# Another set of assumed latencies for the list scheduler of a two-layer attention and MLP kernel, and a condition and a priority in its tail

One Trainium2 chip, one core. The metric is the device time of the whole program in microseconds (us), the median of several executions; lower is better. The profile is of one execution and gives a span some 1.8 us shorter than that execution's device time.

## The reference

Two layers, each attention and then an MLP, on one sequence of 2048 tokens of width 512; 32 heads of 16; hidden width 1792; all tensors bf16.

```python
def _A_ref(x, wqkv, wo):                       # H = 32, Dh = 16
    qkv = (x @ wqkv).reshape(B, S, 3, H, Dh)...
    p = softmax(einsum("bhqd,bhkd->bhqk", q, k) * Dh ** -0.5)
    return einsum("bhqk,bhkd->bhqd", p, v)... @ wo
def _B_ref(x, w1, b1, w2, b2):
    return gelu(x @ w1 + b1) @ w2 + b2          # tanh approximation

x = x + _A_ref(_layernorm(x), A_wqkv, A_wo)     # and _B_ref, both twice
```

Scores are 2 layers x 32 heads x 2048 x 2048, that is 4096 blocks of 128 keys x 512 queries, and each element needs an exponential. That is what the kernel is built around.

## The kernel before

The kernel is a program that writes a program. Threads of work (scores, exponentials, weighted sums of V, LayerNorm, projections, MLP) hand operations with an assumed duration to a list scheduler. It keeps a clock for each engine, and places, again and again, the operation that can start first. The five queues that result, and the semaphores on which they wait, are fixed in the program. "Plan" below is that placement, and "the plan's clock" is the scheduler's own clock: a product of the assumed durations, not a time of the chip.

```python
LATENCY = {"pe": 0.20, "act": 0.10, "dve": 0.10, "pool": 0.15, "sp": 0.1}   # us, end of an op to its reader
MM = 0.2135                                                              # us, one round of 512-column matmuls
...
    for e, cand in best.items():              # _Sched.run: one engine after the other
        now = self.clock[e]
        nowc = [c for c in cand if c[1] <= now]
        if nowc:                              # ready already: priority decides
            ch = min(nowc, key=lambda c: (self._prio(c[0].op), c[0].seq))
        else:                                 # none ready: the earliest
            ch = min(cand, key=lambda c: (c[1], self._prio(c[0].op), c[0].seq))
        ...
    self.clock[e] = start + cost
    self.end[ev] = start + cost + op.tail + LATENCY[e]
```

An exponential on ScalarE takes two or three score blocks from PSUM (`exps`). Blocks of 4 of the 16 key tiles may instead go to DVE, which builds the exponential from integer arithmetic (`dfirst`, `dchain`); whether one does is decided where the plan has a free bank and buffer at that moment. Fillers are matmuls without use that the plan puts into PE's gaps to keep its clock up.

The code is cut at "...", and the comments are added. The tail: the last query chunk is cut in two segments of 256 (tiles 12 and 13, then 14 and 15). After the last exponential ScalarE loads the gelu table and applies gelu to the first segment in two halves; PE has that segment's second MLP matmul (`ytile`, "Y"), the output projection of the second segment (`wo`), and then LayerNorm, MLP and Y of the second one.

```python
    def wo(self, l, seg, t):                                    # output projection of tile t
        ...
        for h in range(0, 4, FQ):                               # two halves, h = 0 and 2
            yield _Op("pe", FQ * MM, ..., prio=MID if h else FPRIO, mode="P")
        yield _Op("dve", DV, ... X += pb ...)
        yield ("give", ("xready", t, 2 * l + 1))

    def ytile(self, l, seg, t):
        tail = l == NL - 1 and seg[0] == self.NQ - 1
        for p in range(1 if (l, seg) == (NL - 1, self.segs[l][-1]) else NFC // 2):
            yield ("need", ("g", l, seg, p))                    # gelu's parts, in the plan
        b = None if tail else (yield ("need", ("w", l, seg, "2", (t, 0))))
        b = yield ("acq", "misc")                               # a PSUM bank
        for p in range(NFC // 2):
            yield ("need", ("g", l, seg, p))
            ...
            yield _Op("pe", len(fns) // 4 * MM, fns, ..., prio=MID if p else FPRIO, mode="P")
        yield _Op("dve", DV, ... X += pb ...)

    # in post(): LayerNorm of the last segment, tile by tile
        for ts in ([t] for t in tiles) if last else (tiles,):
            yield ("spawn", self.ln(ts, xf, xk, LNP, last), LNP)      # LNP = 7
```

The softmax here doesn't subtract the row's maximum and nothing guards it: scores larger than these inputs give would overflow.

## Time and profile before

| | before |
|---|---|
| median of the first 3 runs | 1589.71 us (1587.77 to 1592.41) |
| span of the profile | 1587.3 us |
| ScalarE (ACT) busy | 1547.1 us, 97% |
| last exponential ends | 1560.83 us |
| from there to the end ("the tail") | 26.5 us |

The lines on which this rests stand in the prediction. ScalarE is the bound up to the last exponential; then PE is, for some 21 us.

### The profile page before, as it was taken

The page shows a single profiled execution, that of the slowest core. Times are in us where ns is not written, and L with a number is a line of the kernel's source. Part 1 is how long each engine was busy: PE and PEld are TensorE (multiplying, and loading weights), DVE is VectorE, ACT ScalarE, POOL GpSimd, SP SyncE. Part 2 cuts the span into 40 slices and gives each one's busy share as a digit, 9 for nine tenths or more (in the row PEclk, how much of TensorE's full clock was granted, in tenths as well). Part 3 has the DMA queues.
Part 4 walks back from the last instruction along what each step waited for, and adds up shares of the span by engine and source line. Part 5 has one row for each costly group of instructions (what it writes and reads, how often), then busy time and mean ns, then how long its engine had stood idle before and what let it go on. Part 6 is the DMA issues. An engine that isn't in the chain of part 4 may idle for free.

```text
span 1587.3 us, 42896 instructions
## 1 busy us (share of the span) xinstructions
PE 1424.2 (90%) x18701; PEld 444.6 (28%) x18701; DVE 1352.0 (85%) x2564; ACT 1547.1 (97%) x1393; POOL 200.5 (13%) x250
## 2 busy tenths in 40 slices
PE   8998888899999898988989998888998889898988
PEld 3222222222222222222222222222222222333344
DVE  5689999888898889978788789899878988998984
ACT  7999999999999999999999999999999999999996
POOL 5200012001100201002120020122001000010000
PEclk9999999999999999999999999999999999999999
DMA  5100001241114311143111510001251105312520
GB/s 140 22 2 1 2 14 41 77 132 46 27 45 130 85 41 28 42 140 74 36 28 48 172 44 28 1 2 33 67 167 43 28 15 151 103 36 87 155 82 29
DMA packets 141767, 96.88 MB, mean 61 GB/s; under 512 B 36877, under 2 KB 141582, under 8 KB 141582
## 3 DMA queue, kind: packets, MB, share of 16 engines
q1 hardware_dynamic: 141582, 94.14, 21.2%
q8 instruction: 149, 2.44, 0.6%
q14 instruction: 36, 0.29, 0.1%
HBM read 84.41 MB, written 2.10 MB: 55 GB/s over the span
## 4 chain that ended last, share of the span: by engine, by line
ACT 67%; PE 29%; DVE 2%; POOL 1%; issue 1%; DMA 0%; ACTq 0%; POOLq 0%
ACT pt L1466 60%; PE ps L512 11%; PE ps L1137 9%; PE ps L1527 8%; ACT g L893 3%; ACT v L1466 2%; ACT kt L1466 1%; ACT q L1466 1%; DVE du L1283 1%; ACT L893 1%; ACT L1466 0%; DMA xf<-xln 0%; PE ps L1125 0%; POOL xln L602 0%; POOL rstd L588 0%
## 5 line engine op out<-in xcount | busy, mean ns | idle before, releaser
L1466 ACT ACTIVATE pt<-ps 128x1536 bf16<-128x1536 f32 (+2 forms) x1261 | 1384.2, 1246 | 15.2 <-PE ps L1137 10.3
L1137 PE MATMUL ps<-qp,kt 32*128 32x512 bf16 x4096 | 538.0, 385 | 140.8 <-ACT pt L1466 106.7
L1283 DVE TENSOR_SCALAR du<-ps 128x512 uint16<-128x512 f32 x711 | 479.7, 685 | 97.5 <-PE ps L1137 89.6
L1527 PE MATMUL ps<-pt,v 128*17 128x512 bf16 (+1 forms) x3368 | 433.8, 359 | 2.3 <-ACT pt L1466 0.8
L1527 PE MATMUL ps<-du,vc 128*17 128x512 bf16 (+1 forms) x2394 | 333.8, 358 | 2.7 <-DVE du L1346 1.4
L1137 PEld LDWEIGHTS ps<-qp,kt 32*128 32x128 bf16 x4096 | 140.6, 91 | 685.9 <-ACT pt L1466 304.2
L1346 DVE TENSOR_SCALAR du<-du 128x2048 uint16<-128x2048 uint16 x361 | 246.3, 687 | 2.5
L1085 POOL TENSOR_SCALAR qp<-q,mask 128x512 bf16<-128x512 bf16 (+1 forms) x91 | 66.3, 728 | 1013.8 <-PE ps L1137 1005.1
L512 PE MATMUL ps<-xf,wr 128*32 128x512 bf16 (+1 forms) x2400 | 170.8, 368 | 1.7 <-DMA xf<-xln 1.1
L1527 PE MATMUL ps<-du,v 128*17 128x512 bf16 (+1 forms) x798 | 154.7, 360 | 1.7 <-DVE xt L743 0.9
L1344 DVE TENSOR_SCALAR du<-du 128x1024 uint16<-128x1024 uint16 x361 | 150.5, 428 | 2.0
L1527 PEld LDWEIGHTS ps<-pt,v 128*17 128x17 bf16 x3368 | 111.8, 89 | 113.0 <-issue 72.9
L512 PE MATMUL ps<-wr,g 128*32 128x512 bf16 x1600 | 123.8, 384 | 5.5 <-ACT g L893 5.0
L1527 PEld LDWEIGHTS ps<-du,vc 128*17 128x17 bf16 x2394 | 92.5, 89 | 62.7 <-issue 27.5
L872 DVE TENSOR_SCALAR g<-ps,hb1t 128x512 bf16<-128x512 f32 (+1 forms) x112 | 79.8, 713 | 13.8 <-PE ps L512 12.9
L1527 PE MATMUL ps<-dh,vc 128*17 128x512 bf16 (+1 forms) x321 | 90.6, 358 | 0.0
L1283 DVE TENSOR_SCALAR dh<-ps 128x512 uint16<-128x512 f32 x96 | 65.8, 685 | 11.5 <-PE ps L1137 10.8
L1283 DVE TENSOR_SCALAR kt<-ps 128x512 uint16<-128x512 f32 x82 | 56.1, 684 | 20.7 <-PE ps L1137 19.9
L512 PEld LDWEIGHTS ps<-xf,wr 128*32 128x32 bf16 x2400 | 53.6, 95 | 61.5 <-issue 33.5
L602 POOL TENSOR_SCALAR xln<-x,rstd,nmr 128x512 bf16<-128x512 bf16 x58 | 58.2, 1008 | 33.3 <-DMA xf<-xln 23.2
L754 POOL TENSOR_TENSOR ott<-xt,rc 128x256 bf16<-128x256 f32 x42 | 29.5, 703 | 178.5 <-DVE rc L746 178.5
L1125 PE MATMUL ps<-vc 128*32 128x512 bf16 x476 | 50.9, 395 | 0.1
(93 smaller groups left out, 1185.2 us busy)
## 6 DMA issues: line engine op xcount, KB each, us to landing
wr<-in_B_w_dram SPq DMA_DIRECT2D x256, 256.0 KB, 2.9
wr<-in_A_wqkv_dram SPq DMA_DIRECT2D x24, 256.0 KB, 2.9
wr<-in_A_wo_dram SPq DMA_DIRECT2D x18, 256.0 KB, 2.9
out_dram<-x SPq DMA_DIRECT2D x16, 128.0 KB, 2.7
g<-in_A_wqkv_dram SPq DMA_DIRECT2D x3, 512.0 KB, 5.1
x<-in_A_x_dram SPq DMA_DIRECT2D x3, 512.0 KB, 8.0
q<-in_B_w_dram SPq DMA_DIRECT2D x3, 512.0 KB, 3.9
kt<-in_B_w_dram SPq DMA_DIRECT2D x4, 256.0 KB, 3.3
```

The costliest lines, as they stand in the source:

```text
L512: return [lambda e, a=a: e.matmul(out[32 * a:32 * a + 32, :], lhsT=lhsT[:, 32 * a:32 * a + 32], rhs=rhs, start=start, stop=stop, tile_posi ...
L602: yield _Op(eng, cost, lambda e: e.tensor_scalar(T["XLN"][:, x, :], T["X"][:, t, :], T["RSTD"][:, t:t + 1], T["NMR"][:, t:t + 1], op0=ALU. ...
L872: yield _Op("dve", 0.21 + n / 966, lambda e, fc=fc, pb=pb: e.tensor_scalar(T["G"][:, fc, q], pb, T["HB1T"][:, fc:fc + 1], None, op0=ALU.ad ...
L893: lambda e, g=g: e.activation(out=g, in_=g, func=ACT.Gelu_apprx_tanh), reads=gk, writes=gk, prio=2)
L1085: yield _Op("pool", 0.1 + 0.6 * w / 512, lambda e, s=s, q=q, i=i, t=t, w=w: e.tensor_scalar(T["QP"][:, s, w * i:w * i + w], q, T["MASK"][: ...
L1125: fns.append(lambda e, o=o, w=w, a=a, m=m: e.matmul(o, lhsT=w, rhs=rhs, start=start, stop=start, tile_position=(0, m * a)))
L1137: return (lambda e: e.matmul(o, lhsT=lhsT, rhs=rhs, start=True, stop=True, tile_position=(32 * a, 0)), ["K%d.%d.%d" % (l, gb, kt // 4), "Q ...
L1283: yield _Op("dve", 0.68, lambda e: e.tensor_scalar(u, self.bank(b), E_SCALE, E_BIAS, op0=ALU.mult, op1=ALU.add), reads=["B.%d" % b], write ...
L1344: yield _Op("dve", 0.08 + 0.14 * n, lambda e: e.tensor_scalar(U[:, 1, 0:n, :], U[:, 0, 0:n, :], SHIFT, None, op0=ALU.add), reads=key[0], w ...
L1346: yield _Op("dve", 0.08 + 0.28 * n, lambda e: e.tensor_scalar(U[:, 2:4, 0:n, :], U[:, 0:2, 0:n, :], 2 * SHIFT, None, op0=ALU.add), reads=k ...
L1466: yield _Op("act", 0.065 + 0.4267 * n, lambda e, src=src, dst=dst: e.activation(out=dst, in_=src, func=ACT.Exp, scale=0.25), reads=["B.%d" ...
L1527: op.fns.append(lambda e, o=o, lhsT=q[0][0][m], rhs=q[0][1][:, n * m:n * m + n], a=a, st=st, sp=sp: e.matmul(o, lhsT=lhsT, rhs=rhs, start= ...
```

## The change

Its intent: among forty plans that differ in the assumed latencies, take the one that ends first in a simulated in-order execution; and let Y of the tail open with gelu's first part, with the last LayerNorms ahead of other DVE work.

```diff
-LATENCY = {"pe": 0.20, "act": 0.10, "dve": 0.10, "pool": 0.15, "sp": 0.1}
+LATENCY = {"pe": 0.20, "act": 0.103149, "dve": 0.099491, "pool": 0.153328, "sp": 0.1}
...
-MM = 0.2135
+MM = 0.2132140802823403
...
     def ytile(self, l, seg, t):
-        for p in range(1 if (l, seg) == (NL - 1, self.segs[l][-1]) else NFC // 2):
+        for p in range(1 if tail else NFC // 2):
             yield ("need", ("g", l, seg, p))
...
         for ts in ([t] for t in tiles) if last else (tiles,):
-            yield ("spawn", self.ln(ts, xf, xk, LNP, last), LNP)
+            yield ("spawn", self.ln(ts, xf, xk, LNP, last), 0.2 if last else LNP)
```

## The prediction

> **What bounds the kernel now.** I read the page's first part, then the activity by slices, then the idle of ScalarE by stage, then the chain and the timeline of the last 30 us. The page gives the engine to watch:
>
> ```profile
> PE 1424.2 (90%) x18701; PEld 444.6 (28%) x18701; DVE 1352.0 (85%) x2564; ACT 1547.1 (97%) x1393; POOL 200.5 (13%) x250
> ACT  7999999999999999999999999999999999999996
> ACT 67%; PE 29%; DVE 2%; POOL 1%; issue 1%; DMA 0%; ACTq 0%; POOLq 0%
> ```
>
> ScalarE is busy for 1547.1 of 1587.3 us, so it idles 40.2 us in all, and the slices say that only the first and the last one are visibly short. It is also the engine of two thirds of the chain that ended last. Busy time by stage (columns: stretch; its length and then busy time of PE, PEld, DVE, ACT, POOL, granted clock, DMA share, GB/s):
>
> ```profile
> 0.00:20.00 20.00, 16.86 (x192) 6.45 (x196) 13.45 (x41) 11.74 (x15) 8.56 (x20) 1.00 0.77 237
> 80.00:400.00 320.00, 285.03 (x3435) 80.36 (x3433) 286.07 (x537) 317.91 (x289) 36.04 (x38) 1.00 0.14 39
> 400.00:800.00 400.00, 365.72 (x4514) 105.92 (x4515) 344.64 (x648) 394.47 (x353) 48.77 (x58) 0.99 0.23 64
> 800.00:1200.00 400.00, 353.78 (x4331) 101.84 (x4324) 343.13 (x637) 394.00 (x349) 50.21 (x58) 0.99 0.21 60
> 1200.00:1500.00 300.00, 270.44 (x3897) 93.10 (x3897) 267.72 (x509) 297.22 (x262) 28.45 (x37) 0.99 0.27 77
> ```
>
> ScalarE idle: 8.3 us in the first 20; 2.1, 5.5, 6.0 and 2.8 us in the four stretches of the middle, 16.4 together; and in the last 27 us (1560 to the end at 1587.3) 27.3 less 5.37, 6.30 and 0.47 busy = 15.2 us. With 0.3 us left over between those, that is the 40.2. What makes the middle's idle, by the list of waits (engine, line, releaser; us in total, times, longest):
>
> ```profile
> ACT pt L1466 <- PE ps L1137: 10.3, 25, 0.9
> ACT pt L1466 <- PE ps L1527: 1.3, 1, 1.3
> ```
>
> Some 25 of about 1330 exponentials find their scores not ready, 0.41 us each. The rest of the middle is gaps too small to have a releaser. Then what ScalarE does, by form:
>
> ```profile
> L1466 ACT ACTIVATE pt<-ps 128x1024 bf16<-128x1024 f32 x769 | 798.2, 1080 | 7.4 <-PE ps L1137 6.0
> L1466 ACT ACTIVATE pt<-ps 128x1536 bf16<-128x1536 f32 x491 | 740.2, 1507 | 7.8 <-PE ps L1137 4.2 <-PE ps L1527 1.3
> ```
>
> The difference of the means, 1507 - 1080 = 427 ns, is the price of one score block of 128x512 on ScalarE. Counting all destinations (the same rows for v, kt and q), 540 exponentials hold three blocks, 793 two and 1 one: 3207 blocks. DVE's first steps on score blocks (711 into du, 96 into dh, 82 into kt) are 889, and 3207 + 889 = 4096 = 2 layers x 32 heads x 64 blocks. So the split between ScalarE and DVE is a result of the plan, not a constant: at most 1024 could go to DVE (4 of 16 key tiles), 135 of those fell to ScalarE.
>
> **What the skill says.** "Perfetto Trace Analysis", section "Identifying the Most-Contended Engine", takes occupancy as a fair measure for Scalar and Vector but not for matmuls. The trace agrees in the middle: PE's 90% counts overlapped matmuls and deliberate fillers (476 and 468 of them at L1125), while ScalarE's 97% is the limit. "ScalarE: Activation LUTs", section "What ACT_TABLE_LOAD costs", gives about 1283 ns for the load and about 1380 ns more for a drain, and for an ACTIVATE 186 ns + 0.833 ns per element with about 93 ns overlap with the next. The trace has the load at 1283 ns, but no drain as a gap after it in the tail (load at 1560.83, next ACTIVATE at 1562.12); for the exponentials the formula gives 1039 and 1466 ns against 1080 and 1507 here, the same 427 ns per block. "TensorE: Matmul & The Clock Gate", section "HAM oscillation — how this bites in real kernels", warns of idle gaps over some 3.4 us; PE's clock in this run is 0.99 to 1.00 in every stage, so a plan that keeps the fillers keeps it. No page bears on how a plan reacts to its assumed latencies.
>
> **The change, part 1: the latencies.** ScalarE's assumed signal delay goes from 0.100 to 0.1031 us, DVE's from 0.100 to 0.0995, GpSimd's from 0.150 to 0.1533, and a matmul round from 0.2135 to 0.21321. No instruction becomes faster. These numbers only order the list scheduling, so what changes is the order on the five queues, which blocks go to DVE, and how many exponentials hold two or three blocks. A step of 0.3 to 3 ns in one comparison flips a choice, and every later choice differs: I take it as a fresh draw of the plan, one that was the best of forty in a simulated execution. Its size can be worked out only roughly, and these are my estimates:
> - Waits of ScalarE for scores: 25 of mean 0.41 us. If they come independently, the spread of their sum is about the root of 25 times some 0.5 = 2.5 us.
> - Blocks moved between ScalarE and DVE: DVE has 1587.3 - 1352.0 = 235 us free, and a block costs it about 0.69 + 0.21 + 0.34 = 1.24 us (685 ns per first step; half of 428 and half of 687 ns for the later steps on pairs), so DVE has room; what stops it is free banks at the moment of choice. I assume a spread of 6 blocks out of 889, 6 x 0.427 = 2.6 us.
> - Two or three blocks in one exponential: 1080 - 2 x 427 = 226 ns of visible fixed time, of which consecutive ones overlap most; 1384.2 us busy for 1261 exponentials at 2.39 blocks each leaves about 0.08 us per instruction. Twenty more or fewer are 1.6 us.
> The root of the squares is about 4 us, one draw's spread. The best of forty lies some two spreads below the mean of the score by which it is picked, but that score is not the chip, and the plan before sits among constants tuned around it, so it is probably better than the mean already. I keep about half: one spread, rounded down to 3.5 us gained.
>
> **Part 2: Y opens with gelu's first part.** The two Y tiles of the last but one segment no longer wait in the plan for gelu's second half. The timeline of the tail:
>
> ```profile
> 1562.12 3.28 ACT L893 ACTIVATE g<-g 128x1792 bf16<-128x1792 bf16 x2
> 1563.67 1.05 PE L512 MATMUL ps<-wr,otn 128*32 128x512 bf16 x16 [1.33 <-DVE otn L759]
> 1564.53 2.78 PE L512 MATMUL ps<-q,g 128*32 128x512 bf16 x48
> ```
>
> The first half ends at about 1562.12 + 1.69 = 1563.81 (1688 ns each), the second at 1565.40. Y's first matmuls already run at 1564.53, 0.87 us ahead of the second half's end, because on the chip each waits only for its own part of gelu; the old condition held a plan decision, not an engine. The output projection occupies PE from 1563.67 to 1564.53. PE's one gap, 1.33 us before 1563.67, ends 0.14 us before the first gelu part exists. So this part can gain at most a swap of order: 0 to 0.2 us.
>
> **Part 3: priority 0.2 for the last LayerNorms.** Tiles 14 and 15:
>
> ```profile
> 1566.95 0.27 DVE L586 TENSOR_SCALAR varr<-mv 128x1 f32<-128x1 f32 x2
> 1568.01 0.69 DVE L925 TENSOR_TENSOR x<-x,ps 128x512 bf16<-128x512 bf16 x1 [0.78 <-PE ps L512]
> 1568.61 0.15 DVE L591 SCALAR_TENSOR_TENSOR nmr<-mv,rstd 128x1 f32<-128x1 f32 x1
> ```
>
> Y's addition (0.69 us) stands ahead of the normalisation's step; put behind, the transposes could come about 0.6 us sooner than 1569.62. But PE is then occupied with Y13 anyway, and from 1563.67 to 1584.48 it has no gap worth naming: 20.8 us of work, whose order moves but whose sum doesn't. After it come the last addition (0.69 us) and the store, about 2 us. I give this part 0.2 us; where the last gelu's data arrive a little sooner (the weight load waited 0.2 us for it) it may be a bit more.
>
> Sum: 3.5 + 0.1 + 0.2 = 3.8 us from 1589.7, so 1585.9.
>
> **Rivals.**
> - *The new plan only fits its own assumptions.* The exponentials' waits for scores may grow: twice as many of them are +10.3 us, so about 1600. Against it: forty were tried and the simulated execution runs in order, as the engines do. For it: a wait of 0.4 us is smaller than what a simulation knows of the chip's durations.
> - *More blocks on DVE.* Twenty more would take 8.5 us from ScalarE and put 25 us on DVE, which has 235 free: about 1581. For it: 135 eligible blocks were left to ScalarE. Against: those are left where a bank or a buffer is missing, which the constants don't change.
> - *The tail is worth more.* If Y could fill the 1.33 us gap, the end would come 1.3 us earlier; gelu's end at 1563.81 speaks against. If the plan sent work before the last exponential instead, at most the 15.2 us of ScalarE's tail idle are in play, but PE's 20.8 us are real matmuls that wait on the last attention output.
> - *Nothing at all*: the repeats of before span 1587.77 to 1592.41, so a gain of 3 us would hardly be seen above them.
>
> **Range and chances.** All idle of the middle is 16.4 us, 1.0%; a gain of 2% is 31.8 us and would need all of that and another 36 blocks moved to DVE. A loss of 2% would need four times today's score waits. Neither follows from delays changed by at most 3 ns. Eight times in ten I expect 1579 to 1591.5: about 1.3 spreads to one side, a little more on the slow side for the repeats. Within 2%: 0.97; faster 0.02; slower 0.01.
>
> **What would show it.** Right: ScalarE at 97% as before, counts of two- and three-block exponentials and of DVE's first steps changed by units to tens, its waits for scores within 5 to 16 us, and the saving equal to blocks moved x 0.427 plus the change of idle in the middle. In the tail, from the last exponential to the end still 26 to 26.6 us (now 1560.83 to 1587.3), the LayerNorm's steps ahead of Y's addition, PE gapless. Wrong: a tail shorter by over 1 us, which would mean that order in PE's 20.8 us matters; more than 20 blocks moved; or a filler pattern that lets the clock fall below 0.99.

## More of the kernel before

One more view, PE's timeline in the tail of the kernel before (start, us, engine, line, operation, out<-in, count, idle before it and who ended it), is needed later. Before them stands ScalarE's load of the gelu table, which begins where the last exponential ends. The lines not shown are further matmuls of Y.

```profile
1560.83 1.28 ACT L893 ACT_TABLE_LOAD   x1
...
1567.77 1.91 PE L512 MATMUL ps<-q,g 128*32 128x512 bf16 x32
1569.62 0.62 PE L613 MATMUL ps<-ident,xln 128*128 128x128 bf16 x8
1570.17 1.05 PE L512 MATMUL ps<-q,g 128*32 128x512 bf16 x16
...
1571.69 3.23 PE L512 MATMUL ps<-xf,kt 128*32 128x256 bf16 x112
```

LayerNorm's transposes (`ident,xln`) lie in the middle of Y13 (`q,g`), so PE works on while ScalarE and DVE copy their result, and the MLP (`xf,kt`) follows without a gap.

## The result, and the profile after

| | before | after |
|---|---|---|
| median (6 runs each) | 1588.74 us (1587.05 to 1592.41) | 1586.22 us (1583.84 to 1588.17) |
| ratio | | 0.9982, 95% interval 0.9966 to 0.9998 |
| last exponential ends | 1560.83 us | 1555.12 us |
| tail | 26.5 us | 29.2 us |
| score blocks on DVE | 889 | 889 |
| exponentials of three, two, one block | 540, 793, 1 | 541, 792, 0 |

Ratios here are the mean time of one kernel's fast runs over that of the other's of the same rounds, so not quite the ratio of the medians quoted. The time is within 2%, a small gain just clear of noise, and 0.3 us from the prediction. But two things moved, in opposite directions: the last exponential came 5.7 us earlier in these two profiles, and the tail became 2.7 us longer. The first of these numbers is rough: new_lat_old_tail below has the queues of the changed kernel, and in its profile the last exponential ends 2.6 us later than here. The tail is the same in both, 29.2 us.

First the body. The page of the changed kernel:

```profile
PE 1432.2 (90%) x18795; PEld 447.9 (28%) x18795; DVE 1355.7 (86%) x2558; ACT 1545.8 (98%) x1392; POOL 200.9 (13%) x250
```

ScalarE's list of waits, and its two large forms:

```profile
ACT pt L1466 <- PE ps L1137: 6.4, 14, 1.8
ACT pt L1466 <- PE ps L1527: 1.5, 2, 1.3
```

```profile
L1466 ACT ACTIVATE pt<-ps 128x1024 bf16<-128x1024 f32 x771 | 806.9, 1092 | 3.0 <-PE ps L1137 2.1
L1466 ACT ACTIVATE pt<-ps 128x1536 bf16<-128x1536 f32 x493 | 750.0, 1521 | 7.4 <-PE ps L1137 4.3 <-PE ps L1527 1.5
```

14 exponentials wait for their scores now, for 6.4 us together, against 25 and 10.3. ScalarE's work is the same: 541 x 3 + 792 x 2 = 3207 blocks again. The middle by stage:

```profile
80.00:400.00 320.00, 287.96 (x3424) 82.06 (x3424) 285.18 (x532) 316.85 (x289) 33.25 (x38) 1.00 0.14 40
400.00:800.00 400.00, 368.26 (x4594) 105.82 (x4590) 351.36 (x657) 398.59 (x358) 51.92 (x58) 1.00 0.23 63
800.00:1200.00 400.00, 357.87 (x4399) 103.92 (x4399) 354.04 (x658) 396.85 (x352) 49.90 (x59) 1.00 0.21 61
1200.00:1500.00 300.00, 270.89 (x3944) 93.08 (x3942) 260.41 (x488) 295.96 (x259) 28.71 (x36) 0.99 0.28 79
```

ScalarE's idle time is 3.2, 1.4, 3.2 and 4.0 us where it was 2.1, 5.5, 6.0 and 2.8: less in two stages, more in two others. I see no mechanism that runs through it; it is another order of the same work.

Then the tail: ScalarE's table load, and PE's timeline after (`wr,otn` is the output projection, `q,g` Y, `ident,xln` the transposes):

```profile
1555.12 1.28 ACT L893 ACT_TABLE_LOAD   x1
...
1558.26 1.48 PE L512 MATMUL ps<-q,g 128*32 128x512 bf16 x24 [1.41 <-ACT g L893]
1559.55 0.62 PE L512 MATMUL ps<-wr,otn 128*32 128x512 bf16 x8
1559.98 1.48 PE L512 MATMUL ps<-q,g 128*32 128x512 bf16 x24
...
1561.92 0.62 PE L512 MATMUL ps<-wr,otn 128*32 128x512 bf16 x8
1562.36 2.78 PE L512 MATMUL ps<-q,g 128*32 128x512 bf16 x48
...
1567.09 0.92 PE L613 MATMUL ps<-ident,xln 128*128 128x128 bf16 x8 [1.31 <-DVE xln L602]
...
1568.62 3.24 PE L512 MATMUL ps<-xf,kt 128*32 128x256 bf16 x112 [0.28 <-DVE xf L621]
```

Before, all 16 remaining matmuls of the output projection ran first. Now 24 of Y precede the first 8, and all of Y12 the second 8, at 1561.92. The residual additions that wait for them, and with them LayerNorm, come that much later; all of Y13 (48 matmuls) is used up by then, and PE stands idle for 1.31 us before the transposes and has only four fillers to run beside the copies after them. From the start of the transposes to the next useful matmuls (the MLP now, the rest of Y13 before) it takes 1568.62 - 1567.09 = 1.53 us against 1570.17 - 1569.62 = 0.55 us before. 1.31 + 0.98 = 2.29 us, nearly all of the tail's growth; another 0.30 us is that PE's stretch begins 3.14 us after the last exponential and not 2.84.

Is the new order due to the edit of Y's condition or to the new constants? Programs can be compared without a chip. Built with the old constants, the LayerNorm priority alone gives a byte-identical program. The condition on Y changes neither any queue's order nor any wait, only which PSUM bank a few matmuls of the tail use. With the new constants it is the same: with the edits or without, the same queues. So the order in the tail comes from the constants. In the plan before, the attention output is ready at 1549.549 on the plan's clock and gelu's first half at 1549.568; in the new plan gelu's half is ready at 1545.622 and the attention output at 1545.836. It is a near tie which fell to the other side. The plan's own clock shows the price: built again without a chip, the changed kernel's plan ends at 1569.75, and at 1567.36 with the output projection first (the next experiment), 2.4 us apart.

### The profile page after: what moved, and what is told of

It reads as the page before. It is cut to its first block, busy times and chain, and to the rows that moved or that the text cites. A ratio compares the mean times of both kernels' runs of the same rounds, so it can differ in the third digit from the quotient of the medians.

```text
span 1584.3 us, 43090 instructions
## 1 busy us (share of the span) xinstructions
PE 1432.2 (90%) x18795; PEld 447.9 (28%) x18795; DVE 1355.7 (86%) x2558; ACT 1545.8 (98%) x1392; POOL 200.9 (13%) x250
## 4 chain that ended last, share of the span: by engine, by line
ACT 65%; PE 30%; DVE 2%; POOL 1%; DMA 1%; issue 1%; SPq 0%; POOLq 0%; ACTq 0%
ACT pt L1466 58%; PE ps L512 12%; PE ps L1137 9%; PE ps L1527 9%; ACT g L893 2%; ACT v L1466 1%; ACT kt L1466 1%; ACT q L1466 1%; DVE du L1283 1%; ACT L893 1%; PE ps L1125 1%; DMA xf<-xln 1%; DVE du L1346 0%; ACT L1466 0%; DVE du L1344 0%
## 5 line engine op out<-in xcount | busy, mean ns | idle before, releaser
L1466 ACT ACTIVATE pt<-ps 128x1536 bf16<-128x1536 f32 (+1 forms) x1264 | 1387.1, 1259 | 10.5 <-PE ps L1137 6.4
L1527 PE MATMUL ps<-pt,v 128*17 128x512 bf16 (+1 forms) x3386 | 444.9, 359 | 3.2 <-DVE v L739 1.1
L1527 PE MATMUL ps<-du,vc 128*17 128x512 bf16 (+1 forms) x2403 | 326.6, 359 | 1.3 <-DVE du L1344 0.6
L1346 DVE TENSOR_SCALAR du<-du 128x2048 uint16<-128x2048 uint16 (+1 forms) x361 | 246.7, 686 | 2.2
L1344 DVE TENSOR_SCALAR du<-du 128x1024 uint16<-128x1024 uint16 (+1 forms) x361 | 152.6, 433 | 2.2
L1527 PE MATMUL ps<-du,v 128*17 128x512 bf16 (+1 forms) x801 | 148.3, 360 | 0.8 <-DVE du L1346 0.5
L1527 PEld LDWEIGHTS ps<-pt,v 128*17 128x17 bf16 x3386 | 114.4, 88 | 114.8 <-issue 76.6
L1527 PEld LDWEIGHTS ps<-du,vc 128*17 128x17 bf16 x2403 | 91.0, 89 | 65.4 <-issue 30.2
L1527 PE MATMUL ps<-dh,vc 128*17 128x512 bf16 (+1 forms) x309 | 86.4, 357 | 0.0
L1125 PE MATMUL ps<-vc 128*32 128x512 bf16 x520 | 54.7, 384 | 0.0
L754 POOL TENSOR_TENSOR ott<-xt,rc 128x256 bf16<-128x256 f32 x42 | 33.3, 792 | 164.3 <-DVE rc L746 158.8
```

Of the source, the lines that this page charges most:

```text
L1125: fns.append(lambda e, o=o, w=w, a=a, m=m: e.matmul(o, lhsT=w, rhs=rhs, start=start, stop=start, tile_position=(0, m * a)))
L1344: yield _Op("dve", 0.08 + 0.14 * n, lambda e: e.tensor_scalar(U[:, 1, 0:n, :], U[:, 0, 0:n, :], SHIFT, None, op0=ALU.add), reads=key[0], w ...
L1346: yield _Op("dve", 0.08 + 0.28 * n, lambda e: e.tensor_scalar(U[:, 2:4, 0:n, :], U[:, 0:2, 0:n, :], 2 * SHIFT, None, op0=ALU.add), reads=k ...
L1466: yield _Op("act", 0.065 + 0.4267 * n, lambda e, src=src, dst=dst: e.activation(out=dst, in_=src, func=ACT.Exp, scale=0.25), reads=["B.%d" ...
L1527: op.fns.append(lambda e, o=o, lhsT=q[0][0][m], rhs=q[0][1][:, n * m:n * m + n], a=a, st=st, sp=sp: e.matmul(o, lhsT=lhsT, rhs=rhs, start= ...
```

## The experiments

My theories after the result: (A) the tail's order costs the 2.7 us; (D) each set of constants is a fresh draw of the body's order, and the chip follows the plan's clock. Their rivals stand in the expectations. The diffs below are shortened to their sense.

### after_wo_first: the changed kernel with the output projection first

```diff
 wo:
+        yield ("give", ("wo", l, seg, t))
         yield _Op("dve", DV, ... X += pb ...)
 ytile:
+        end = self.segs[l][-1]
+        if tail and seg != end: need ("wo", l, end, u) for u in self.tiles(end)
         b = None if tail else (...)
```

> The changed kernel with one edit: in the plan, Y of the last but one segment is offered only once both output projections of the last segment are placed; on the engines' queues only the order of PE and DVE work in the last 27 us differs. Theory A (the tail is longer after the change, 29.2 us from the last exponential to the end against 26.5, because PE's queue has Y ahead of the second half of the output projection, which delays the LayerNorm and leaves PE idle before the transposes): tail back to 26.3 to 26.8 us, PE's 1.31 us wait before the transposes gone, time 2 to 2.7 us under the changed kernel's, about 1583.7. Rival B (the tail is longer because the new plan's last attention pass ends differently, and PE's sum of work is what counts, as the prediction had it): tail stays 29 us, time 1586.

Measured: 1584.11 us median (1581.11 to 1585.13), ratio to before 0.9962 (0.9950 to 0.9973). The last exponential ends at 1553.12, the span at 1579.8: tail 26.7 us. PE's timeline:

```profile
1556.18 1.05 PE L512 MATMUL ps<-wr,otn 128*32 128x512 bf16 x16 [1.33 <-DVE otn L759]
1557.04 2.78 PE L512 MATMUL ps<-q,g 128*32 128x512 bf16 x48
...
1562.12 0.62 PE L613 MATMUL ps<-ident,xln 128*128 128x128 bf16 x8
1562.67 1.05 PE L512 MATMUL ps<-q,g 128*32 128x512 bf16 x16
...
1564.19 3.23 PE L512 MATMUL ps<-xf,kt 128*32 128x256 bf16 x112
```

The transposes have Y13 on both sides again, and the gap before them is gone. Theory A holds. This version is faster than the kernel before, though within 2%; against the changed kernel see new_lat_old_tail, which ran in the same rounds.

### before_y_first: the mirror image on the kernel before

```diff
 wo, before each half:
+        if h and seg is the last one: need ("yp", l, 12, 2 if t == 14 else 6)
 ytile, after each step:
+            yield ("give", ("yp", l, t, p))
```

> The mirror image on the kernel before: the second halves of the output projection are put behind Y's first three and all seven steps, as the changed plan has it; nothing else differs up to the last exponential. Theory A: the tail grows from 26.5 to about 29 us, PE idles 1.3 us before the transposes, time 2 to 2.7 us over before, about 1591. Rival B: tail stays 26.5 us, time as before.

Measured: 1591.12 us median (1589.88 to 1593.60), ratio 1.0012 (1.0000 to 1.0024); last exponential 1559.75, span 1588.9, tail 29.2 us.

```profile
1571.72 0.91 PE L613 MATMUL ps<-ident,xln 128*128 128x128 bf16 x8 [1.31 <-DVE xln L602]
1572.56 0.40 PE L1125 MATMUL ps<-vc 128*32 128x512 bf16 x4
1573.24 3.24 PE L512 MATMUL ps<-xf,kt 128*32 128x256 bf16 x112 [0.28 <-DVE xf L621]
```

The same gaps of 1.31 and 0.28 us appear in a plan whose body is untouched. Rival B, my own reading that PE's sum is all that counts, is out in both directions. The ratio's 1.9 us are a little under the 2.7 of the two profiles; its interval (0 to 3.8 us) holds both that and no change, so it is the profiles that show the effect here. On the plan's clock this kernel ends 2.6 us later than before.

### new_lat_old_tail: the constants alone

The edit: the two lines of constants of the change, and nothing else of it.

> The kernel before with the new assumed latencies and matmul time alone; the condition on Y and the LayerNorm's priority are as before. Its queues hold the same instructions in the same order with the same waits as the changed kernel's; only some matmul outputs in the tail use another PSUM bank. Theory A (both tail edits change nothing that takes time): within 1 us of the changed kernel, about 1586, tail about 29.2 us. Rival C (the edits had an effect, a loss in the tail): tail 26.5 us, time about 1583.5.

Measured: 1588.28 us median (1584.81 to 1588.71), ratio 0.9985 (0.9973 to 0.9997), where the changed kernel had 0.9982; last exponential 1557.74, span 1586.9, tail 29.2 us. The median is 2.3 us above the 1586 I had written, so the expectation of "within 1 us" was missed; but that was another chip job, and by ratio the two agree. The tail is what tells: 29.2 us, not 26.5, so rival C is out and the two edits of the tail cost and bring nothing. In the same rounds the mean is 1587.5 us against 1583.5 for after_wo_first: some 4 us apart, of which the tails explain 2.5; the rest is within the spread of six runs each.

### draw_179_wo_first: the best of 320 draws on the plan's clock

I drew 320 sets of constants (each latency within 4%, the matmul time within 0.2%) and read the plan's clock at the end of DVE's last operation. With the output projection first their mean is 1576.9 and their standard deviation 3.8; before ends at 1571.1, after_wo_first at 1567.4, the best draw at 1567.2. (160 fresh ones gave 1577.0 and 3.3; 6 of them ended before 1571.1.)

```diff
-LATENCY = {..., "act": 0.103149, "dve": 0.099491, "pool": 0.153328, ...};  MM = 0.2132140802823403
+LATENCY = {..., "act": 0.103212, "dve": 0.097585, "pool": 0.153896, ...};  MM = 0.213123
```

The expectation names other constants than the kernel that ran. The diff shows those that ran, and their plan is the one described: built again, it ends at 1567.2 with 900 blocks on DVE. The constants in the expectation give 1567.7 and 898.

> As after_wo_first, with other assumed latencies (ScalarE 0.102332, DVE 0.096248, GpSimd 0.154053, matmul 0.213344), the plan of 320 random draws whose own clock ends earliest: 1567.2 against 1567.4 for after_wo_first and 1571.1 for before. It puts 900 score blocks on DVE against 889. Theory D (the chip follows the plan's clock to 3 us or so): 1581 to 1586, and ScalarE 4.7 us less busy for the 11 blocks. Rival E (the plan's clock does not order plans this close, each draw is luck): anywhere from 1580 to 1592.

Measured: 1586.12 us median (1582.62 to 1587.35), ratio 0.9973 (0.9961 to 0.9986). ScalarE's busy time is 1542.7 us, 3.1 less than after the change; 11 blocks x 0.427 would be 4.7, and it has 5 instructions more. But it waits longer: from 20 us to the last exponential it idles 15.1 us against 10.4 in after_wo_first. The list of waits of this kernel has a line (the second here) that before, after and after_wo_first lack:

```profile
ACT pt L1466 <- PE ps L1137: 4.8, 17, 0.6
ACT v L1466 <- PE ps L1527: 3.6, 3, 1.8
```

So in this plan more blocks on DVE, a rival of the prediction, take work from ScalarE, and the time is lost again to waits, 3.6 us of them for buffers that the weighted sums (L1527) free. The median is 0.1 us above the range of theory D, and the ratio (1585.0 us) within it; its interval overlaps that of after_wo_first, so the plan's clock did not order two plans 0.1 us apart.

### Parts of the change as draws of their own

Each is the kernel before with the output projection first (which, on it, changes no queue) and one edit of the constants. lat_only_wo_first:

```diff
-LATENCY = {"pe": 0.20, "act": 0.10, "dve": 0.10, "pool": 0.15, "sp": 0.1}
+LATENCY = {"pe": 0.20, "act": 0.103149, "dve": 0.099491, "pool": 0.153328, "sp": 0.1}
```

> The kernel before with the three new latencies but the old matmul time, tail order fixed (output projection first). Its plan ends on its own clock at 1573.2, with 892 blocks on DVE; the plans run so far ended on the chip 16 to 19 us after their own clock (1571.1 gave 1589.3, 1567.4 gave 1584.1, 1567.2 gave 1586.1). Theory D (each set of constants is a fresh draw, and the chip follows the plan's clock within some 2 us): 1589 to 1593, so slower than before although it holds most of the change's constants. Rival F (the new latencies are better in themselves, nearer to the chip's): 1583 to 1587, as the changed kernel.

Measured: 1593.53 us median (1591.74 to 1595.09), ratio 1.0025 (1.0010 to 1.0040), 0.5 us above the range of theory D. mm_only_wo_first:

```diff
-MM = 0.2135
+MM = 0.2132140802823403
```

> The kernel before with the new matmul time alone, tail order fixed. Its plan ends at 1581.2 on its own clock, 886 blocks on DVE. Theory D: 1597 to 1601, ratio about 1.006. Rival F (the matmul time is the better constant): 1583 to 1587. Rival E (the chip does not follow the plan's clock, differences are luck): anywhere, most likely 1584 to 1592.

Measured: 1598.60 us median (1595.69 to 1603.65), ratio 1.0061 (1.0039 to 1.0083), within theory D. Each half of the constants is slower than before; the two together are faster. Rival F (the constants are better in themselves) is out for both. mm_nudge_wo_first:

```diff
-MM = 0.2135
+MM = 0.21349
```

> The kernel before with the matmul time 0.21349 in place of 0.2135, 0.01 ns less[...]; tail order fixed. Its plan ends at 1576.8, with 882 blocks on DVE. Theory D (fresh draw): 1593 to 1597. Rival G (a small change of a constant makes a small change of time): 1589, as before.

Measured: 1592.76 us median (1591.46 to 1593.41), ratio 1.0020 (1.0005 to 1.0035): a hundredth of a nanosecond in an assumption makes 3 us on the chip (0.20% of 1589 us; 0.8 to 5.6 us by the interval). The median is 0.2 us under the range that theory D gave, and the ratio is clear of rival G. Its plan puts 7 blocks fewer on DVE, and here this term of the prediction does act: from 20 us to the last exponential ScalarE is busy 3.4 us longer than before (7 x 0.427 = 3.0) and idles 1.1 us more.

### draw_98_wo_first: the worst of 320 draws

```diff
-LATENCY = {"pe": 0.20, "act": 0.103149, "dve": 0.099491, "pool": 0.153328, "sp": 0.1};  MM = 0.2132140802823403
+LATENCY = {"pe": 0.20, "act": 0.098851, "dve": 0.102649, "pool": 0.148229, "sp": 0.1};  MM = 0.213123
```

> The worst of 320 random draws on the plan's clock: 1592.4 (ScalarE 0.098851, DVE 0.102649, GpSimd 0.148229, matmul 0.213123), 887 blocks on DVE, tail order fixed. Theory D: 1607 to 1612, ratio 1.012 to 1.015, with some 20 us more of ScalarE idle in the middle. Rival E: 1584 to 1595.

Measured: 1607.85 us median (1607.03 to 1609.99), ratio 1.0120 (1.0103 to 1.0137). ScalarE's waits and the timeline where the largest one lies:

```profile
ACT pt L1466 <- PE ps L1527: 16.2, 6, 11.6
ACT pt L1466 <- PE ps L1137: 12.0, 29, 1.3
```

```profile
1503.50 7.57 ACT L1466 ACTIVATE v<-ps 128x1536 bf16<-128x1536 f32 x6
1522.63 11.57 ACT L1466 ACTIVATE pt<-ps 128x1536 bf16<-128x1536 f32 x10 [11.56 <-PE ps L1527]
```

One gap of 11.56 us: the exponentials have no free buffer until PE's weighted sums release one. The chain of this kernel leads in that gap through the weight loads of Y and of the output projection (3.40 and 3.49 us) and the last steps of a segment. From 20 us to the last exponential ScalarE is busy for 1525.4 us, against 1524.1 before, and idles 33.0 us, against 16.8. Of the 18.2 us by which this profile is longer, 16.2 are that idle (some 20 were expected).

### The draws together

| kernel (all with the output projection first) | plan's clock | blocks on DVE | ratio to before |
|---|---|---|---|
| draw_179 | 1567.2 | 900 | 0.9973 |
| after_wo_first | 1567.4 | 889 | 0.9962 |
| before | 1571.1 | 889 | 1 |
| lat_only | 1573.2 | 892 | 1.0025 |
| mm_nudge | 1576.8 | 882 | 1.0020 |
| mm_only | 1581.2 | 886 | 1.0061 |
| draw_98 | 1592.4 | 887 | 1.0120 |

With the ratio times 1589.3 us the chip's time correlates with the plan's clock at 0.98, slope 0.95, and the farthest point is 2.6 us off the line; without draw_98 the correlation is 0.96. Rival E is out over a range of 25 us; within 2 or 3 us of one another the plan's clock doesn't sort.

## Why the prediction was right, and where it was not

The number was right by luck: two errors of opposite sign cancelled.

- **What bounds the kernel, and the class of the change.** Right. ScalarE stays at 97 to 98%, and the constants make no instruction faster. "A fresh draw of the plan" is shown by the nudge and by the two halves of the constants. The spread I estimated, about 4 us, agrees with 3.8 on the plan's clock; that the plan before was better than the mean already also holds, 1571.1 against 1576.9.
- **Part 1, 3.5 us from the latencies.** Right in kind and too small. The body was profiled twice with the old constants (last exponential at 1560.83 and 1559.75) and three times with the new (1555.12, 1553.12, 1557.74): 5.0 us earlier by the means, though profiles of the same queues differ by 2.6. The device times agree: gain by the ratio plus growth of the tail is 5.6 us for the changed kernel, 6.2 for after_wo_first and 5.1 for new_lat_old_tail. Of my three terms, blocks moved to DVE gave nothing (889 and 889) and the sizes of exponentials nothing (1334 instructions and 1333). The term of waits gave it all: ScalarE's idle time from 20 us to the last exponential is 16.8 and 15.5 us before, and 12.0, 10.4 and 14.0 after, 4.0 less on average. The remaining 1.0 us is in what counts as busy, and I did not find its cause.
- **Part 2, 0 to 0.2 us.** Nothing, and so within its range. Right about the edit, by its own reasoning: the condition held a plan decision and no engine, and no queue's order changes.
- **Part 3, 0.2 us.** Nothing: the same program, byte for byte. The priority is asked only among operations that are ready at the same moment. In the new plan, Y13's addition takes DVE at 1553.071, before GpSimd's result lets LayerNorm's step start; the trace after has them in that order too, 1565.83 and 1566.43.
- **The step that failed:** "20.8 us of work, whose order moves but whose sum doesn't", and with it the tail "still 26 to 26.6 us" and "PE gapless". The sum is what PE works; the tail is what it works plus what it waits, and the order sets the wait. With Y in front, PE's stretch is 1558.26 to 1581.41 = 23.15 us against 20.81, before_y_first has 23.15 too, and after_wo_first 20.80 again. I had named a tail shorter by over 1 us as the sign that order matters; it was longer by 2.7.
- **The rivals of the prediction.** "More blocks on DVE" is possible (draw_179) and its gain partly returns as waits. "The new plan only fits its own assumptions" is refuted, as the chip follows the plan's clock. "Nothing at all" is only just excluded by the changed kernel itself (upper end of the interval 0.9998), and clearly by after_wo_first.
- **Two slips in the working.** From 1585.9 the range reaches 6.9 us to the fast side and 5.6 to the slow side, 1.7 and 1.4 spreads of 4 us; so it is not "a little more on the slow side". And GpSimd's delay changed by 3.3 ns, more than "at most 3 ns". Nothing rests on either.

What stays open: runs with the new constants had a somewhat higher mean granted clock (0.9945 to 0.9958 in three groups of 6) than those of before (0.9929 and 0.9937 in groups of 11 and 7). The new program has 94 more PE instructions; scores and projections are the same in number, and the fillers (L1125) are 1064 against 964. But their number does not sort the clock: mm_nudge has 920 at a mean clock of 0.9945, lat_only 1036 at 0.9920; nor does the clock sort the kernels, as draw_98, the slowest, has 0.9958. By the correlation in the last section, 0.002 of clock goes with some 1.5 us, an estimate. Whether the plan raised the clock, and so made part of the 5 us, was not tried.

## What to carry to other kernels

Where a static plan comes out of a greedy scheduler, treat its constants as a random seed: draw many, rank them by the plan's own clock, and (by the seven plans here) believe that ranking for differences over 3 us only. Before crediting an edit of such a planner, compare the programs it emits; two of the four edits here emit the same queues. In a tail that one engine fills, look at what its order delays elsewhere: work that feeds a long chain on other engines goes first, and independent work is kept to lie beside that chain.

## What the Trainium skill lacked or had wrong

- "ScalarE: Activation LUTs", section "What ACT_TABLE_LOAD costs", adds some 1380 ns of drain to the load's 1283 ns. In the tail the load is 1283 ns and the gelu follows at once in every profile: 1555.12 + 1.28, next ACTIVATE at 1556.42 after the change; 1560.83 and 1562.12 before. There is no gap before the load either: after the change the last exponentials run to 1549.53 + 5.58 = 1555.11.
- The same section's overlap of about 93 ns between ACTIVATEs leaves 186 - 93 = 93 ns of fixed time for each. Here 1264 exponentials of the group pt on 3021 blocks are busy for 1387.1 us; less 3021 x 0.427 that is 77 ns each, an estimate from that row.
- "TensorE: Matmul & The Clock Gate", section "HAM oscillation — how this bites in real kernels", tells of the clock in large steps. No page says that small differences of the mean granted clock go with the run-to-run spread: over 63 runs of 11 groups, with clocks of 0.990 to 0.999, each 0.001 less went with 0.75 us more within a group (for before in one job, 1587.1 us at 0.996 and 1591.74 at 0.990). That is a correlation, not a shown cause.
- No page bears on how far a program's time depends on the order of a static plan: 1584 to 1608 us here for the same work.
